# Second MLP of an attention-and-two-MLPs kernel: its matmuls in long runs, its inputs prepared without GpSimd

## The chip, the cores and the metric

The kernel runs on one core of one Trainium2 chip. The time is that of one launch on the device, in microseconds (us), the median of several executions. Engines are called PE or TensorE (matmuls), PEld (TensorE's weight loads, which overlap the matmuls), DVE or VectorE, ACT or ScalarE, POOL or GpSimd, and SP or SyncE, which here only issues DMAs.

## The reference

Attention through a packed set of 32 queries per head, then two MLPs on the 4608 x 512 result, all in float32:

```python
out = sm_attn(q, p_packed, p_packed)          # p_packed = sm_attn(p, k, v); 8 batches, 8 heads, 576 x 64
x = out as (4608, 512)
h = x @ moe_w_in                              # (512, 2048)
x = where(h >= 1, h, where(h <= -1, 0, (h + 1) ** 2 / 4)) @ moe_w_out
h = x @ moe2_w_in                             # second MLP: (512, 2048)
out = (h * 1 / (1 + exp(-h))) @ moe2_w_out    # (2048, 512)
```

The weights come as 64-bit floats, and the kernel turns them into 32-bit ones itself. A float32 product is made of three TensorE passes, each factor being split into a high and a low part (high x high, high x low, low x high).

## The kernel before

**Stages.** Attention and the first MLP run in 256 steps (NA = 256), a step being one (batch, half, column block m) triple: `a_h` makes the hidden block (6 matmuls of 288 columns, L544), four steps ahead of its use; `a_relu`, `a_max`, `a_hi`, `a_lo` make its activation g on ScalarE and VectorE (L552 to L568); `a_y` multiplies it into the output (12 matmuls, L578). The result goes to DRAM as y_dram. Then comes the second MLP.

**The second MLP** works on six blocks of 2 x 384 tokens and, in each, on eight pairs of hidden column blocks; a pair of a block is numbered q, 0 to 47. The hidden values of a pair are a 2 x 2 block product, done with seven products in place of eight. Product j (0 to 6) of pair q is `b_product`: 6 matmuls of 384 columns (L702), a2r (a prepared piece of the first weights, loaded from a_dram by `load_a` on SyncE's queue) times y2 (a prepared side of the block's tokens, made by `b_side` and `split_b`). Products 0, 2, 4 and 6 are written to one PSUM bank, 1, 3 and 5 to another; products 2, 5 and 6 add to what the bank holds, the others start it anew. So between two products on one bank the chain must have read it: `c_sum` (L715 on ScalarE for p1, L722 on VectorE for u2, u3, c22, c21 and c12), or for c11 the sigmoid and the multiply, which read the bank directly. Each of the four hidden blocks c11, c22, c21, c12 then takes a sigmoid (`c_sig`, L728, ScalarE), a multiply (`c_mult`, L733, VectorE), and a split into high (`c_hi`, L737, ScalarE) and low part (`c_lo`, L742, VectorE).

The output product of a pair, `b_out`, has 36 matmuls of 512 columns (L756), into six banks that gather over the eight pairs of a block; at the last pair they are copied to osb tiles and written out. Before the change it is cut into seven parts of 5 or 6 matmuls, and part j of pair q stands behind product j of pair q + 1.

**The second output weights** (key "o2") are read as raw 64-bit words (`load_raw`, SyncE), scaled on ScalarE (`conv_a`, L162), put together on VectorE (`conv_b`, L168 and L169) and split by `conv_c`: ScalarE makes the high part (L206), GpSimd the low part (L207). Before the change nine of the 16 go through from step NA - 10 on, the others every fourth place. The first weights of the second MLP (key "i2") are prepared much earlier, a pair at a time, from step ai = 24 on, every ad = 27 steps, by `conv_a`, `conv_b` and `a_first` to `a_fourth`.

**What sets the order.** Every operation is put down as an event with a number (`ev`, or `at`, which adds 0.6), and the events are written out in the order of these numbers; each engine's queue then runs in that order. kb(q, j) is the place of product j of pair q, one unit a product. The seven low parts of block 0's y2 tiles are made by GpSimd (L664), those of later blocks by VectorE.

## Time and profile before

| | us |
|---|---|
| median of three executions | 1579.46 |
| lowest, highest | 1578.46, 1586.15 |
| profiled execution, whole | 1583.54 |
| its span, first to last instruction | 1581.8 |
| TensorE busy in the span | 1536.6 (97%) |
| VectorE, ScalarE busy | 1041.8 (66%), 683.5 (43%) |
| GpSimd busy | 124.3 (8%) |
| share of TensorE in the chain that ended last | 85% |

TensorE is the engine that is nearly always busy. Matmuls are pipelined: the recorded duration of one reaches beyond the start of the next, so a busy TensorE can still start its matmuls at a faster or a slower rate. How far apart they start has to be read from the order of time: the starts of two rows, or a row's length less one matmul, divided by its count less one.

### The profile page before, as it was taken

What the parts mean: (1) busy time and instruction counts of PE and PEld (TensorE: products, weight loads), DVE (VectorE), ACT (ScalarE), POOL (GpSimd) and SP (SyncE); (2) the same over time, 40 slices, a digit from 0 to 9 for tenths busy, and PEclk for the clock granted to TensorE, in tenths of its full rate; (3) what the DMA queues carried; (4) which work ended last, traced back from release to release, by engine and by line L of the source; (5) the groups of instructions that cost most, each with busy time, mean ns of one, the idle gap of its engine ahead of it and who ended that gap; (6) DMA issues with size and microseconds to landing.
All of it is one profiled execution on the core that took longest, in us unless ns stands there. A gap on an engine that the chain in (4) does not pass through costs nothing.

```text
span 1581.8 us, 26920 instructions
## 1 busy us (share of the span) xinstructions
PE 1536.6 (97%) x10110; PEld 1404.6 (89%) x10110; DVE 1041.8 (66%) x2105; ACT 683.5 (43%) x1479; POOL 124.3 (8%) x138
## 2 busy tenths in 40 slices
PE   6899999999999999999979999999999999999998
PEld 4687899989999999999969988988998998988897
DVE  5998779776868588767685465465456456447444
ACT  4565456454544455534454343243233234224222
POOL 1431310000000000000251000000000000000000
PEclk7999999999999999999999999999999999999999
DMA  9545675183424544213435445355355455455432
GB/s 335 180 171 167 226 254 156 45 248 98 131 97 128 168 143 138 89 43 102 149 124 177 127 146 157 118 157 156 118 155 156 117 160 154 119 155 150 124 118 87
DMA packets 140433, 231.15 MB, mean 146 GB/s; under 512 B 25104, under 2 KB 71184, under 8 KB 140304
## 3 DMA queue, kind: packets, MB, share of 16 engines
q1 hardware_dynamic: 133392, 204.26, 41.0%
q0 software_dynamic: 6912, 25.17, 5.1%
q8 instruction: 81, 1.33, 0.4%
q14 instruction: 48, 0.39, 0.1%
...
## 4 chain that ended last, share of the span: by engine, by line
PE 85%; DVE 9%; ACT 2%; DMA 2%; issue 1%; SPq 0%; POOL 0%; DVEq 0%; ACTq 0%; POOLq 0%
PE ps_o L756 23%; PE ps_y L578 23%; PE ps_h L702 21%; PE ps_h L544 11%; PE ps_wp L514 2%; PE ps_s L375 2%; DVE raw L168 1%; DVE u L557 1%; DVE w L169 1%; PE ps_s L264 1%; DVE u L558 1%; PE ps_pp L338 1%; DVE g L568 1%; DVE w_in L169 1%; DVE y L664 1%
## 5 line engine op out<-in xcount | busy, mean ns | idle before, releaser
L578 PE MATMUL ps_y<-g,w_o 128*128 128x288 f32 x3072 | 462.8, 300 | 9.2 <-DVE g L568 7.3
L756 PE MATMUL ps_o<-w_o,g 128*128 128x512 f32 x1728 | 452.1, 393 | 0.0
L578 PEld LDWEIGHTS ps_y<-g,w_o 128*128 128x128 f32 x3072 | 429.4, 191 | 25.4 <-DVE g L568 8.6
L702 PE MATMUL ps_h<-y,a2r 128*128 128x384 f32 x2016 | 411.2, 339 | 2.9 <-ACT p L715 1.5
L702 PEld LDWEIGHTS ps_h<-y,a2r 128*128 128x128 f32 x2016 | 365.1, 188 | 32.9 <-ACT p L715 5.0
L756 PEld LDWEIGHTS ps_o<-w_o,g 128*128 128x128 f32 x1728 | 319.3, 188 | 47.9
L544 PE MATMUL ps_h<-a,wp 128*128 128x288 f32 x1536 | 248.0, 298 | 4.9 <-DVE u L558 3.9
L552 ACT ACTIVATE u<-ps_h,half 128x288 f32<-128x288 f32 x256 | 128.0, 502 | 257.0 <-PE ps_h L544 192.0
L544 PEld LDWEIGHTS ps_h<-a,wp 128*128 128x128 f32 x1536 | 219.7, 190 | 8.6 <-DVE u L558 5.5
L557 DVE SCALAR_TENSOR_TENSOR u<-u 128x288 f32<-128x288 f32 x256 | 124.3, 486 | 105.7 <-ACT u L552 105.0
L728 ACT ACTIVATE s<-c 128x384 f32<-128x384 f32 x144 | 75.7, 526 | 192.5 <-DVE c L722 192.4
L737 ACT CAST g<-s 128x384 fp32r<-128x384 f32 x192 | 98.5, 513 | 107.4 <-DVE s L733 106.5
L722 DVE TENSOR_TENSOR c<-ps_h,u 128x384 f32<-128x384 f32 x144 | 80.0, 555 | 76.0 <-PE ps_h L702 76.0
L558 DVE TENSOR_TENSOR u<-ps_h,u 128x288 f32<-128x288 f32 x256 | 117.1, 457 | 8.8
L742 DVE TENSOR_TENSOR g<-s,g 128x384 fp32r<-128x384 f32 x192 | 107.5, 560 | 23.3 <-ACT g L737 22.5
L562 ACT CAST g<-u 128x288 fp32r<-128x288 f32 x256 | 109.0, 427 | 19.2 <-DVE u L558 18.3
L568 DVE TENSOR_TENSOR g<-u,g 128x288 fp32r<-128x288 f32 x240 | 116.4, 485 | 0.5
L733 DVE TENSOR_TENSOR s<-c,s 128x384 f32<-128x384 f32 x144 | 80.4, 558 | 47.9 <-ACT s L728 47.9
L728 ACT ACTIVATE s<-ps_h 128x384 f32<-128x384 f32 x48 | 23.6, 492 | 136.9 <-PE ps_h L702 136.8
L733 DVE TENSOR_TENSOR s<-ps_h,s 128x384 f32<-128x384 f32 x48 | 26.7, 557 | 75.9 <-ACT s L728 75.7
L529 DVE TENSOR_TENSOR wp<-ps_wp,wp 64x512 fp32r<-64x512 f32 x96 | 65.7, 687 | 12.5 <-ACT wp L527 10.8
L722 DVE TENSOR_TENSOR u<-ps_h,p 128x384 f32<-128x384 f32 x48 | 26.6, 555 | 54.1 <-PE ps_h L702 54.1
...
## 6 DMA issues: line engine op xcount, KB each, us to landing
a2r<-a_dram SPq DMA_DIRECT2D x336, 256.0 KB, 2.6
...
a_dram<-a2w SPq DMA_DIRECT2D x56, 256.0 KB, 3.5
...
```

What stands on the lines that cost most here:

```text
L544: nc.tensor.matmul(ps[:, :HB], w[:, i, o:o + P], a2[:, k, g, :], start=(n == 0), stop=(n == 3 * NG - 1))
L552: nc.scalar.activation(u, h_ps[s][:, :HB], AF.Relu, bias=half, scale=0.5)
L557: nc.vector.scalar_tensor_tensor(u, u, 1.0, u, op0=ALU.min, op1=ALU.mult)
L558: nc.vector.tensor_tensor(u, h_ps.pop(s)[:, :HB], u, op=ALU.max)
L562: nc.scalar.copy(g[:, 0], u_t[s])
L568: eng.tensor_tensor(g[:, 1], u_t.pop(s), g[:, 0].bitcast(F32), op=ALU.subtract)
L578: nc.tensor.matmul(acc["y"][d][:, :HB], w[:, i, d * P:(d + 1) * P], g[:, k], start=(first and n == 0), stop=(last and n == 2),)
L702: nc.tensor.matmul(ps, w[:, x, a * P:(a + 1) * P], y[:, k, :], start=(n == 0 and j in (0, 1, 3, 4)), stop=(n == 3 * KH - 1), skip_group_ch ...
L722: nc.vector.tensor_tensor(t, ps, sb[q, other], op=ALU.add)
L733: nc.vector.tensor_tensor(u, src, u, op=ALU.mult)
L742: nc.vector.tensor_tensor(g[:, 1], c_t.pop((q, name))[0], g[:, 0].bitcast(F32), op=ALU.subtract)
L756: nc.tensor.matmul(ps, g[:, x, c * P:(c + 1) * P], w[:, k, :], start=(first and (x, k) == PASSES[0]), stop=(last and (x, k) == PASSES[-1]),)
```

## The change

The output product of a pair is no longer cut up: all 36 matmuls stand behind product 3 of the next pair, so TensorE has products 4, 5, 6 of one pair and 0, 1, 2, 3 of the next as one run of 42, and then a run of 36. Its cells come in another order, both halves of one t after each other. The chain's operations are placed anew among the products. Products 0 to 3 of the first pair now stand between the last four output steps of the first MLP. Low parts of y2 and of the second output weights are made by VectorE throughout. Only four output weights are converted ahead of the second MLP, the others in pairs, each in the output run of an earlier pair; so are the sides of later blocks. The first weights are prepared from step 34 on, every 25 steps. Loads are placed accordingly.

```diff
-        nc.gpsimd.tensor_tensor(t[:, 1], w, t[:, 0].bitcast(F32), op=ALU.subtract)
+        eng = nc.gpsimd if key[0] == "o" else nc.vector
+        eng.tensor_tensor(t[:, 1], w, t[:, 0].bitcast(F32), op=ALU.subtract)
...
-        if n < 7:
+        if n < 5:
             t = big.tile([P, 2, KH * P], F32R, tag="big", name="a2r")
...
-            (eng or nc.vector).tensor_tensor(t[:, 1], src[:, a], t[:, 0].bitcast(F32), op=ALU.subtract)
+            nc.vector.tensor_tensor(t[:, 1], src[:, a], t[:, 0].bitcast(F32), op=ALU.subtract)
...
-        u = tmp("s", 2)
+        u = tmp("s", 3)
...
-    def b_out(q, part):
+    def b_out(q):
         i, p = divmod(q, NPR)
-        cells = [(f, t, c, x) for f, t in ((0, 0), (1, 1), (1, 0), (0, 1)) for c in range(TC) for x in PASSES]
-        n = len(cells)
-        for f, t, c, (x, k) in cells[n * part // 7:n * (part + 1) // 7]:
+        order = ((0, 0), (1, 0), (1, 1), (0, 1)) if q + 1 < NPR * NBK else ((0, 0), (1, 1), (1, 0), (0, 1))
+        cells = [(f, t, c, x) for f, t in order for c in range(TC) for x in PASSES]
+        for f, t, c, (x, k) in cells:
...
-                osb = pools["b"].tile([P, DM], F32, tag="osb", name="osb", bufs=3)
-                if c % 2:
+                if t and c < 2 and q + 1 < NPR * NBK:
+                    osb = big.tile([P, DM], F32, tag="big", name="osb")
+                else:
+                    osb = pools["b"].tile([P, DM], F32, tag="osb", name="osb", bufs=3)
+                if c == 1 or c == 2 and t:
...
-            n = NA - 10 + m if m < 9 else NA - 2 + (m - 8) * 4
+            n = NA - 8 + m if m < 4 else kb(m // 2 - 1) + 3.5
...
-            return NA - 1 + 7 * q + j
+            return NA - 3.95 + 7 * q + j
...
-                at(NA - 15 + 2 * j if i == 0 else n - 7 + 1.4 * j, b_side, i, j)
+                if i == 0:
+                    at(NA - 26 + 3 * j, b_side, i, j)
+                else:
+                    ev(n + 7 * (-2, -1, -1, -1, 0, 0, 0)[j] + 3.6 + 0.01 * j, b_side, i, j)
...
-            ev(kb(0, n) - 4 + 0.39, load_a, n)
+            ev(kb(0, n) - (3 if n < 5 else 4.6) + 0.39, load_a, n)
...
                 ev(kb(q, j) + 0.37, b_product, q, j)
-                ev(kb(q + 1, j) + 0.9, b_out, q, j)
+            ev(kb(q + 1, 3) + 0.9, b_out, q)
```

The chain's table (`chain`) is rewritten too; what it does to VectorE's order is shown below.

TensorE, the last pair but one, before: the last three products of pair 47 (L702; ps_h is the bank, y the token side) with parts of pair 46's output product (L756; g is the hidden block) between them.

```order
L756 MATMUL ps_o<-w_o_13_10531,g_16646 128x512 x3
L756 MATMUL ps_o<-w_o_13_10531,g_16669 128x512 x2
L702 MATMUL ps_h_16658<-y_15681,a2r 128x384 x3
L702 MATMUL ps_h_16658<-y_15684,a2r 128x384 x3
L756 MATMUL ps_o<-w_o_13_10531,g_16669 128x512 x5
L702 MATMUL ps_h_16680<-y_15727,a2r 128x384 x3
L702 MATMUL ps_h_16680<-y_15730,a2r 128x384 x3
L756 MATMUL ps_o<-w_o_13_10531,g_16669 128x512 x2
L756 MATMUL ps_o<-w_o_12_10442,g_16689 128x512 x3
L702 MATMUL ps_h_16658<-y_15757,a2r 128x384 x3
L702 MATMUL ps_h_16658<-y_15760,a2r 128x384 x3
L756 MATMUL ps_o<-w_o_12_10442,g_16689 128x512 x6
```

The same place after the change, from pair 47's product 2 on.

```order
L702 MATMUL ps_h_16658<-y_15617,a2r 128x384 x3
L702 MATMUL ps_h_16658<-y_15620,a2r 128x384 x3
L702 MATMUL ps_h_16673<-y_15624,a2r 128x384 x3
L702 MATMUL ps_h_16673<-y_15627,a2r 128x384 x3
L756 MATMUL ps_o<-w_o_12_10834,g_16582 128x512 x9
L756 MATMUL ps_o<-w_o_13_10837,g_16683 128x512 x9
L756 MATMUL ps_o<-w_o_13_10837,g_16654 128x512 x9
L756 MATMUL ps_o<-w_o_12_10834,g_16696 128x512 x9
L702 MATMUL ps_h_16658<-y_15760,a2r 128x384 x3
L702 MATMUL ps_h_16658<-y_15763,a2r 128x384 x3
L702 MATMUL ps_h_16673<-y_15767,a2r 128x384 x3
L702 MATMUL ps_h_16673<-y_15770,a2r 128x384 x3
```

Between a product and the next one on the same bank there is now a single product, except at the output run.

VectorE, one pair of the second MLP before, from u2 on (L722 sums, L733 multiplies, L742 low parts, by the pair's tiles).

```order
L722 TENSOR_TENSOR u2_12095<-ps_h2_12066,p1_12077 128x384
L733 TENSOR_TENSOR s_12112<-ps_h2_12044,s_12112 128x384
L722 TENSOR_TENSOR u3_12130<-ps_h2_12066,u2_12095 128x384
L742 TENSOR_TENSOR g2_12132<-s_12112,g2_12132 128x384
L722 TENSOR_TENSOR c_12150<-ps_h2_12044,u3_12130 128x384
L733 TENSOR_TENSOR s_12152<-c_12150,s_12152 128x384
L722 TENSOR_TENSOR c_12168<-ps_h2_12066,u2_12095 128x384
L742 TENSOR_TENSOR g2_12170<-s_12152,g2_12170 128x384
L733 TENSOR_TENSOR s_12172<-c_12168,s_12172 128x384
L722 TENSOR_TENSOR c_12191<-ps_h2_12044,u2_12095 128x384
L742 TENSOR_TENSOR g2_12193<-s_12172,g2_12193 128x384
L733 TENSOR_TENSOR s_12195<-c_12191,s_12195 128x384
```

The same engine after the change, from sum c22 on: c_12754 is c22, c_12766 c21, c_12782 c12, and u2_12810 belongs to the next pair.

```order
L722 TENSOR_TENSOR c_12754<-ps_h2_12645,u3_12697 128x384
L722 TENSOR_TENSOR c_12766<-ps_h2_12660,u2_12680 128x384
L733 TENSOR_TENSOR s_12756<-c_12754,s_12756 128x384
L722 TENSOR_TENSOR c_12782<-ps_h2_12645,u2_12680 128x384
L733 TENSOR_TENSOR s_12768<-c_12766,s_12768 128x384
L742 TENSOR_TENSOR g2_12771<-s_12756,g2_12771 128x384
L733 TENSOR_TENSOR s_12784<-c_12782,s_12784 128x384
L722 TENSOR_TENSOR u2_12810<-ps_h2_12790,p1_12797 128x384
L742 TENSOR_TENSOR g2_12800<-s_12768,g2_12800 128x384
L742 TENSOR_TENSOR g2_12813<-s_12784,g2_12813 128x384
```

Multiplies and low parts have moved behind the sums that free a bank.

TensorE in the passage before: the last output steps of the first MLP (L578) and the first products.

```order
L578 MATMUL ps_y<-g,w_o_1227 128x288 x12
L578 MATMUL ps_y<-g,w_o_1230 128x288 x12
L578 MATMUL ps_y<-g,w_o_1360 128x288 x12
L578 MATMUL ps_y<-g,w_o_1373 128x288 x12
L702 MATMUL ps_h_10088<-y_9638,a2r 128x384 x3
L702 MATMUL ps_h_10088<-y_9641,a2r 128x384 x3
L578 MATMUL ps_y<-g,w_o_1309 128x288 x12
```

The same place after the change (there the line is L579).

```order
L579 MATMUL ps_y<-g,w_o_1227 128x288 x12
L702 MATMUL ps_h_10003<-y_9336,a2r 128x384 x3
L702 MATMUL ps_h_10003<-y_9339,a2r 128x384 x3
L579 MATMUL ps_y<-g,w_o_1230 128x288 x12
L702 MATMUL ps_h_10032<-y_9423,a2r 128x384 x3
L702 MATMUL ps_h_10032<-y_9426,a2r 128x384 x3
L579 MATMUL ps_y<-g,w_o_1360 128x288 x12
L702 MATMUL ps_h_10003<-y_9507,a2r 128x384 x3
L702 MATMUL ps_h_10003<-y_9510,a2r 128x384 x3
L579 MATMUL ps_y<-g,w_o_1373 128x288 x12
```

A product now stands between each two of the last output steps.

## Rows read from the trace of the kernel before

**Rows 1.** Busy us by stretch: PE, PEld, DVE, ACT, POOL; then granted clock, DMA.

```profile
750.00:780.00 30.00, 30.00 (x228) 30.00 (x227) 17.65 (x40) 11.68 (x30) 2.30 (x3) 1.00 0.32 114
...
796.90:826.60 29.70, 20.23 (x110) 18.24 (x109) 25.31 (x37) 16.65 (x32) 17.02 (x13) 0.89 0.34 111
...
800.00:820.00 20.00, 12.89 (x70) 11.75 (x70) 17.47 (x25) 10.96 (x22) 12.62 (x10) 0.83 0.12 37
...
827.70:1565.20 737.50, 736.81 (x3645) 661.62 (x3645) 395.09 (x732) 255.53 (x515) 7.84 (x6) 1.00 0.47 141
```

**Rows 2.** TensorE in order of time, one period: start, us, line, tiles, count.

```profile
1205.08 1.21 PE L702 MATMUL ps_h<-y,a2r 128*128 128x384 f32 x6
...
1215.00 1.32 PE L756 MATMUL ps_o<-w_o,g 128*128 128x512 f32 x5
...
1220.83 1.21 PE L702 MATMUL ps_h<-y,a2r 128*128 128x384 f32 x6
```

**Rows 3.** TensorE in order of time, longer runs of products and of outputs.

```profile
824.53 2.07 PE L702 MATMUL ps_h<-y,a2r 128*128 128x384 f32 x11
...
1566.25 9.72 PE L756 MATMUL ps_o<-w_o,g 128*128 128x512 f32 x42
...
1568.56 7.42 PE L756 MATMUL ps_o<-w_o,g 128*128 128x512 f32 x32
```

**Rows 4.** TensorE, passage: one y step, then groups (busy, mean ns, idle before, releaser).

```profile
792.14 1.77 PE L578 MATMUL ps_y<-g,w_o 128*128 128x288 f32 x12
...
L578 PE MATMUL ps_y<-g,w_o 128*128 128x288 f32 x60 | 11.3, 344 | 7.3 <-DVE g L568 7.3
L702 PE MATMUL ps_h<-y,a2r 128*128 128x384 f32 x48 | 9.6, 346 | 2.2 <-ACT p L715 1.1 <-DMA a2r<-a_dram 0.6 <-DVE s L733 0.5
```

**Rows 5.** VectorE and ScalarE in order of time, in the period of rows 2.

```profile
1215.20 0.56 DVE L722 TENSOR_TENSOR c<-ps_h,u 128x384 f32<-128x384 f32 x1 [1.19 <-PE ps_h L702]
1216.41 0.56 DVE L733 TENSOR_TENSOR s<-c,s 128x384 f32<-128x384 f32 x1 [0.65 <-ACT s L728]
1217.42 0.56 DVE L722 TENSOR_TENSOR c<-ps_h,u 128x384 f32<-128x384 f32 x1 [0.45 <-PE ps_h L702]
1217.89 0.55 DVE L742 TENSOR_TENSOR g<-s,g 128x384 fp32r<-128x384 f32 x1
...
1215.85 0.52 ACT L728 ACTIVATE s<-c 128x384 f32<-128x384 f32 x1 [3.40 <-DVE c L722]
```

**Rows 6.** All engines in order of time, first products.

```profile
816.84 0.42 DVE L168 TENSOR_SCALAR raw<-raw 128x512 uint32<-128x512 uint32 x1
...
817.39 0.69 DVE L169 SCALAR_TENSOR_TENSOR w<-raw 128x512 uint32<-128x512 uint32 x1
...
820.90 0.56 DVE L733 TENSOR_TENSOR s<-ps_h,s 128x384 f32<-128x384 f32 x1 [1.63 <-ACT s L728]
...
821.51 1.01 PEld L702 LDWEIGHTS ps_h<-y,a2r 128*128 128x128 f32 x6 [0.86 <-DVE s L733]
```

**Rows 7.** Order of time, a weight load that waited and its matmul.

```profile
956.59 0.49 PEld L702 LDWEIGHTS ps_h<-y,a2r 128*128 128x128 f32 x3 [0.15 <-ACT p L715]
...
956.71 0.52 PE L702 MATMUL ps_h<-y,a2r 128*128 128x384 f32 x2
```

**Rows 8.** DMA issues: KB each, median us from issue to landing.

```profile
a2r<-a_dram SPq DMA_DIRECT2D x336, 256.0 KB, 2.6
```

**Rows 9.** Groups on VectorE from 780 to 826: busy, mean ns, idle before.

```profile
L169 DVE SCALAR_TENSOR_TENSOR w<-raw 128x512 uint32<-128x512 uint32 x10 | 11.4, 1138 | 0.9
```

**Rows 10.** Order of time, an early conversion and TensorE's wait behind it.

```profile
158.44 1.02 DVE L168 TENSOR_SCALAR raw<-raw 128x512 uint32<-128x512 uint32 x1
159.49 0.69 DVE L169 SCALAR_TENSOR_TENSOR w<-raw 128x512 uint32<-128x512 uint32 x1
...
162.53 1.12 PE L306 MATMUL ps_et<-ident,s 128*128 128x128 f32 x4 [2.88 <-DVE u L558]
```

More of the change, by code (lines that the diff above doesn't have):

```diff
@@ L658, in load_y, with split_b @@
         yr_t[i, k, t] = yr
-    def split_b(i, j, src, eng=None):
+    def split_b(i, j, src):
         for a in range(KH):
@@ L663, in split_b @@
             nc.scalar.copy(t[:, 0], src[:, a])
-            (eng or nc.vector).tensor_tensor(t[:, 1], src[:, a], t[:, 0].bitcast(F32), op=ALU.subtract)
+            nc.vector.tensor_tensor(t[:, 1], src[:, a], t[:, 0].bitcast(F32), op=ALU.subtract)
             b_t[i, j, a] = t
     def b_side(i, j):
-        eng = nc.gpsimd if i == 0 else nc.vector
         b11, b12, b21, b22 = (yr_t[i, k, t] for k in range(2) for t in range(2))
         if j == 0:
-            split_b(i, 0, b11, eng)
+            split_b(i, 0, b11)
             nc.vector.tensor_tensor(b11, b12, b11, op=ALU.subtract)
@@ L675, in b_side @@
             nc.vector.tensor_tensor(t2, b22, b11, op=ALU.subtract)
-            split_b(i, 1, t2, eng)
+            split_b(i, 1, t2)
             yr_t[i, "t2"] = t2
         elif j == 2:
-            split_b(i, 2, b21, eng)
+            split_b(i, 2, b21)
         elif j == 3:
             nc.vector.tensor_tensor(b12, b22, b12, op=ALU.subtract)
-            split_b(i, 3, b12, eng)
+            split_b(i, 3, b12)
         elif j == 4:
-            split_b(i, 4, b11, eng)
+            split_b(i, 4, b11)
         elif j == 5:
             nc.vector.tensor_tensor(b21, b21, yr_t[i, "t2"], op=ALU.subtract)
-            split_b(i, 5, b21, eng)
+            split_b(i, 5, b21)
         else:
-            split_b(i, 6, b22, eng)
+            split_b(i, 6, b22)
     bk, sb, c_t = {}, {}, {}
@@ L708, in tmp @@
     def tmp(name, bufs):
-        return pools["b"].tile([P, TH], F32, tag=name, name=name, bufs=bufs)
+        return pools["y" if name == "p1" else "b"].tile([P, TH], F32, tag=name, name=name, bufs=bufs)
     def c_sum(q, name):
@@ L772, in b_out @@
                     s0 += m
[L775 removed]
+    G = dict(pf1=4, pb1=18, w1=2, sp0=25, spd=125, pf2=25, pf3=41, pb2=44, pp2=52, t20=52, t21=58, t22=57, t23=65, pbo=7, pfa=18, pfb=25, pbe=40, pp=36, t0=37, t1=53, t2=49, t3=66, lw=3, lk=4, lv=-1, lq=21, ppd=0, ai=34, ad=25, wpd=1, bev=4, oraw=1)
     starts = {b: (0,) if b else (0, KF // 2) for b in range(B)}
@@ L978, in attention_then_two_mlps @@
         at(NA - SPB, start_b)
-        at(NA - 2, end_a)
+        ev(NA - 1.6, end_a)
         for p in range(NPR):
@@ L988, in attention_then_two_mlps, with kb @@
                 at(n + 8 + x, fn, p)
+        def kb(q, j=0):
+            return NA - 3.95 + 7 * q + j
         for m in range(KF):
             key = ("o2", m)
-            n = NA - 10 + m if m < 9 else NA - 2 + (m - 8) * 4
-            at(n - 3, load_raw, key)
-            at(n, conv_a, key)
-            at(n + 1, conv_b, key)
-            at(n + 2, conv_c, key)
-        def kb(q, j=0):
-            return NA - 1 + 7 * q + j
+            n = NA - 8 + m if m < 4 else kb(m // 2 - 1) + 3.5
+            ev(n - 4, load_raw, key)
+            ev(n, conv_a, key)
+            ev(n + (1 if m < 4 else 0.02), conv_b, key)
+            ev(n + (2 if m < 4 else 0.04), conv_c, key)
         for i in range(NBK):
@@ L1003, in attention_then_two_mlps @@
                 for t in range(2):
-                    at((NA - 22 if i == 0 else n - 13) + 2 * k + t, load_y, i, k, t)
+                    ev((NA - 31.4 if i == 0 else n - 22) + 2 * k + t, load_y, i, k, t)
             for j in range(7):
-                at(NA - 15 + 2 * j if i == 0 else n - 7 + 1.4 * j, b_side, i, j)
+                if i == 0:
+                    at(NA - 26 + 3 * j, b_side, i, j)
+                else:
+                    ev(n + 7 * (-2, -1, -1, -1, 0, 0, 0)[j] + 3.6 + 0.01 * j, b_side, i, j)
         for n in range(7 * NPR * NBK):
-            ev(kb(0, n) - 4 + 0.39, load_a, n)
+            ev(kb(0, n) - (3 if n < 5 else 4.6) + 0.39, load_a, n)
         chain = {
-            1: [(c_sum, "p1")],
-            2: [(c_sum, "u2")],
-            3: [(c_sig, "c11"), (c_mult, "c11")],
-            4: [(c_sum, "u3"), (c_hi, "c11"), (c_lo, "c11")],
-            5: [(c_sum, "c22"), (c_sig, "c22"), (c_mult, "c22")],
-            6: [(c_sum, "c21"), (c_hi, "c22"), (c_sig, "c21"), (c_lo, "c22"), (c_mult, "c21")],
-            7: [(c_sum, "c12"), (c_hi, "c21"), (c_sig, "c12"), (c_lo, "c21"), (c_mult, "c12")],
-            8: [(c_hi, "c12"), (c_lo, "c12")],
+            1: [(c_sum, "p1", 0)],
+            2: [(c_sum, "u2", 0)],
+            3: [(c_sig, "c11", 0), (c_mult, "c11", 1), (c_sum, "u3", 2), (c_hi, "c11", 3), (c_lo, "c11", 4)],
+            5: [(c_sum, "c22", 0), (c_sig, "c22", 1)],
+            6: [(c_sum, "c21", 0), (c_sig, "c21", 1), (c_mult, "c22", 2), (c_hi, "c22", 3)],
+            7: [(c_sum, "c12", 0), (c_sig, "c12", 1), (c_mult, "c21", 2), (c_lo, "c22", 3)],
+            8: [(c_mult, "c12", 1), (c_hi, "c21", 2)],
+            9: [(c_lo, "c21", 1), (c_hi, "c12", 2), (c_lo, "c12", 3)],
         }
@@ L1021, in attention_then_two_mlps @@
                 ev(kb(q, j) + 0.37, b_product, q, j)
-                ev(kb(q + 1, j) + 0.9, b_out, q, j)
+            ev(kb(q + 1, 3) + 0.9, b_out, q)
             for j, fns in chain.items():
-                for x, (fn, name) in enumerate(fns):
+                for fn, name, x in fns:
                     ev(kb(q, j) + 0.4 + 0.01 * x, fn, q, name)
```

1 line of the change is left out of this document (removed).

## The prediction

> **What bounds the kernel now.** I read the stretches first, then the order of time, then the waits. In the stage of the second MLP, 827.7 to 1565.2 us, TensorE is busy 736.81 of 737.50 us at a granted clock of 1.00, with VectorE at 395 and ScalarE at 256 [rows 1]. So the stage is bound by the rate at which matmuls start, and a change there pays only through that rate. A period of 42 product and 36 output matmuls takes 15.75 us, from 1205.08 to 1220.83 [rows 2]; the stage holds 3645 / 78 = 46.7 periods [rows 1], of 737.5 / 46.7 = 15.79 us on average, block borders included.
>
> That rate isn't what long runs reach. Eleven products in a row start (2.07 - 0.33) / 10 = 173.6 ns apart, and 32 output matmuls in a row (7.42 - 0.39) / 31 = 226.8 ns apart [rows 3]. At these spacings 42 + 36 matmuls are 7.29 + 8.16 = 15.45 us, 0.30 less than the period of runs of 6 and 5. The run of 42 at the end, taken from its first matmul, has (9.72 - 0.39) / 41 = 227.6 ns [rows 3]: some 41 x 0.8 ns = 0.03 us are lost once at its head. Runs of 5 or 6 pay such a head 14 times a period.
>
> The other place is the passage from the first MLP to the second. From 796.9 to 826.6 TensorE is busy 20.2 of 29.7 us, at a clock of 0.89, 0.83 in its middle [rows 1]. It does 60 matmuls of 288 and 48 of 384 columns; its idle time is mostly VectorE's g, 7.3 us [rows 4]. At the usual (1.77 - 0.30) / 11 = 0.134 us [rows 4] and 0.174 these are 8.0 + 8.4 = 16.4 us, so the passage loses 13.3.
>
> **The change part by part.** *Runs.* A period becomes 15.45 plus a head for each of two runs, 0.03 (measured) and about as much for the products (taken from the same row), so 15.51 if nothing waits. Before, a product's result had an output part of 1.2 us and a product before its bank was written again; now it has one product of 1.04 us, five times a period. Call the products P4 P5 P6 of one pair and P0 to P3 of the next, and count from the start of P4. Handing over costs: product's end to VectorE 0.20 (1215.00 to 1215.20), sum to sigmoid 0.65, sigmoid to multiply 0.56, VectorE 0.56 an operation and 0.47 from one start to the next where they are independent [rows 2, 5]; a VectorE end to the weight load that waits for it 0.05 (821.46 to 821.51), which I take for ScalarE too, and VectorE to its own dependent successor 0.13 (817.26 to 817.39) [rows 6]. A weight load 0.12 us ahead of its matmul costs it nothing (956.59, 956.71) [rows 7].
> P4 ends at 1.07, P5 at 2.11, P6 at 3.15, then P0 4.19, P1 5.23, P2 6.27, P3 7.31. Sum c22 starts 1.27, frees P6's bank at 1.88; wanted at 1.99. Sum c21: 2.31, 2.92; wanted 3.03. Multiply c22 comes behind c21 at 2.78 and ends 3.34; sum c12 takes over its tile, so it starts between 3.47 and 3.52 and frees P1's bank at 4.08 to 4.13; wanted 4.07. The sigmoid of c12 (4.13) holds ScalarE up to 0.52, so copy p1, priced like it, ends by 5.17 and frees P2's at 5.22, or 0.1 sooner where the two overlap; wanted 5.15. Sum u2 starts 5.47, frees P3's at 6.08; wanted 6.19. So c12, and perhaps p1, is late by 0 to 0.10 in a period. I take 0.04, the middle of c12's, which the durations pin best. P4 and P5 (multiply c11, sum u3) have the output run of 8.2 us as cover.
> *Vector work in the output run.* For the first pairs it holds multiply, sum and low half of c11 (3 x 0.56) and two weights, each 0.42 + 0.69 and a subtraction, which I price at 0.69 as the like-sized operation: 5.3 of 8.2 us. Nothing of it is paid for; were it 3 us longer, sum c22 would be late and each us of it would cost a us. Before a block's border three y sides stand there, 6 x 0.56 + 2 x 0.95 for the wider ones (twice 0.47, by columns) + 1.7 = 7.0: still under. At the borders themselves the periods of before are longer, which is in the 15.79; I leave 1 us of that for the five new borders.
> Sum: 47 x (15.79 - 15.51 - 0.04) = 11.3, less 1: **10.3 us**. Bounds: 0.10 late each period and the borders as before (2 us for 1), 6.5; none late and no border cost, 13.2.
> *Loads on SyncE's queue.* a2r lands 2.6 us after its issue [rows 8]. Five buffers hold P4 to P1; P2's load goes out when P4 ends, at about 1.3, and is there by 3.9 to 4.4 with 0.5 allowed for the issue; wanted 5.15. P3's: 5.4, wanted 6.19. The weights' raw loads stand behind P3's load, ahead of P4's, whose product has the output run to come. The output writes stand at the borders ahead of P2's load only. Cost zero; without that slack of 0.8 us P2 would pay what is missing.
> *Passage.* GpSimd's 14 y subtractions and 16 weight subtractions go to VectorE; 12 of 16 weights leave the passage, and 4 y steps are interleaved with P0 to P3. Ten L169 from 780 to 826 took 1138 ns each [rows 9]; the one at 817.39 took 690 [rows 6], and GpSimd, which ran 17 of the passage's 30 us [rows 1], is what it shares the passage with. A step of 18 matmuls takes TensorE 18 x 0.134 = 2.4 us; VectorE's work in one is 17.65 / 30 x 2.4 = 1.4 (750 to 780 us) [rows 1]. In the four steps that hold weights 0.42 + 0.69 + 0.69 come on top: 3.2 against 2.4, and against 1.6 + 1.04 = 2.65 once a product stands in the step. With three steps of the first kind and one of the second that is a lag of 3 us at full durations, 2 where they overlap by 0.1, and g is wanted a step and a half (3.6 us) after its place. From 0 (all covered) to 5 us (lag uncovered, with the sigmoid table's load) remains; I take 2.5, nearer the middle as the y sides before it fill VectorE already. 13.3 - 2.5 = **10.8 us** (8.3 to 13.3).
> *Pairs of the first weights* (ai, ad). Pair 0 moves some ten steps later. Two of its conversions stand ahead of the u for which TensorE waits 2.88 us until 162.53, the second with 1.02 + 0.69 [rows 10]. Without them that wait shrinks by up to its whole length, but the same work lands elsewhere: between 1.7 lost, where that second conversion meets as tight a place, and 2.9 won; I take **1.7** won, that conversion alone.
> The tail keeps its order: 36 output matmuls after the last product, then copies and writes.
> Total 10.3 + 10.8 + 1.7 = 22.8 us. The profiled execution took 1583.54 (span 1581.8): 1560.7. It lies 4.1 above the median, 1579.46, to which the forecast refers: **1557 us**.
>
> **The rivals.** *The handovers are late.* Five a period x 47 = 235. If each is 0.10 us later than worked out above, after its slack, 23.5 us go back: 1580, no change. For: all five have 0.1 us of slack or less. Against: the durations are steady, and a late one shifts all that follows with it. *Much later*: with 0.25 each 59 us: 1614, slower. It decides from 0.13 each, (1587 - 1557) / 235. It would need VectorE to reach the product run with work left over from the output run.
> *The runs don't settle*: small waits renew the head every product, the spacing stays as now, and only passage and start pay: 1567. For: there are five chances for it in a run. Against: the eleven products in a row cross from P6 to P0 [rows 3].
> *The passage stays VectorE-bound*: it takes over 30 subtractions. With 8 us more left: 1565.
> *The clock falls.* It was 0.83 in 800 to 820, where TensorE waited four times for VectorE's g, 7.3 us in all [rows 1, 4]. If the handover waits did the same to the product runs, 7.3 x (1 / 0.83 - 1) = 1.5 us a period, 70 in all: 1627. Against: it stayed at 1.00 through the stage [rows 1]. The Trainium skill (TensorE: Matmul & The Clock Gate, A second HAM failure mode: psum-queue depth-cycling) reports a kernel whose short idle times between groups of matmuls, while it cycled through banks, made the clock swing; that speaks against this change, and no row of before shows it.
> *Long runs go below the samples*, down to their columns at 2.4 GHz, 160 and 213 ns: 14.4 us a period, 1.05 less, 49 in all: 1508. Rows 3 speak against it, 32 in a row without a further fall. The Trainium skill (the same page, Wait — 56ns, not 53.3ns?) gives columns / 2.4 GHz plus about 2.5 ns as the distance of warm matmuls, which is close to that end; by it the period would be 14.6. The trace disagrees by 11 ns a matmul.
>
> **How the numbers follow.** Forecast 0.75; late by 0.10 (1580) 0.07; much later (1614) 0.04; not settling (1567) 0.08; passage (1565) 0.03; clock (1627) 0.02; below the samples (1508) 0.01. About 0.5%, 7.9 us, is what a measurement of this kernel can tell from no change. Faster by more: 0.75 + 0.08 + 0.03 + 0.01 = 0.87; within: 0.07; slower: 0.06. The range holds the forecast with its bounds and the rivals at 1565 and 1567, and leaves out the rest: low, 1557 less 2.9 (runs), 2.5 (passage) and 1.2 (pairs) = 1550.4, taken as 1551; high 1568, just past the rival at 1567 and the other ends of the three terms, 1557 + 3.8 + 2.5 + 3.4 = 1566.7.
>
> **What would show it.** Right: a period near 15.55 us; rows of 42 products with spacings near 174 ns and 36 outputs near 227; TensorE's idle time in the passage under 3 us with the clock at 1.00 and L169 at 0.69; no GpSimd after the first MLP. Wrong: weight loads that wait for c or p in every period; a period at 15.7 or more; VectorE busy up to the end of the output run; TensorE waiting for g in the last steps of the first MLP; or a new wait between 150 and 250 us.

## The result, and the profile after

The changed kernel takes 1560.63 us, the median of four executions (1559.21 to 1562.29); the kernel before, run beside it, 1581.07. The ratio is 0.987, with a 95% interval of 0.984 to 0.990: 1.0 to 1.6% faster. The prediction was 1557, with a range of 1551 to 1568. The profiled execution took 1560.93, where the prediction had worked out 1560.7 for one beside the profiled 1583.54.

So the total fits almost exactly. Its terms don't. The spans of the two profiled executions can be cut at three matmuls that both have: the first of the last five output steps of the first MLP (step 251), the first of product P4 of pair 0 (behind 60 output matmuls and the 24 of P0 to P3 in either kernel), and the last product matmul.

| us, from the starts in order of time | before | after | gained | predicted |
|---|---|---|---|---|
| start to step 251 (first MLP) | 796.93 | 784.30 | 12.6 | 1.7 |
| step 251 to P4 of pair 0 (passage) | 24.58 | 12.33 | 12.2 | 10.8 |
| P4 of pair 0 to the last product | 744.57 | 747.75 | -3.2 | 10.3 |
| last product to the end | 15.70 | 14.78 | 0.9 | 0 |
| span | 1581.8 | 1559.2 | 22.6 | 22.8 |

Before, 42 output matmuls follow the last product, after the change 36 (the prediction took 36 for both). So six of them, 1.4 us, have moved from the fourth row into the third; for equal work the second MLP is 1.8 us slower and the tail 0.5.

The second MLP, for which the runs were made, came out slower by itself. The first MLP gained what is missing there.

TensorE in the passage after, in order of time (start, us, line, tiles, count). The same place as in [rows 4]:

```profile
784.30 1.77 PE L579 MATMUL ps_y<-g,w_o 128*128 128x288 f32 x12
785.90 1.24 PE L702 MATMUL ps_h<-y,a2r 128*128 128x384 f32 x6
786.98 1.78 PE L579 MATMUL ps_y<-g,w_o 128*128 128x288 f32 x12
...
795.03 1.77 PE L579 MATMUL ps_y<-g,w_o 128*128 128x288 f32 x12
796.63 5.40 PE L702 MATMUL ps_h<-y,a2r 128*128 128x384 f32 x30
```

Every one of these rows begins where the one before it runs out, and none has a wait. A step and a product together take 786.98 - 784.30 = 2.68 us. Busy time by stretch (PE, PEld, DVE, ACT, POOL; then granted clock, DMA share, GB/s), which answers [rows 1]:

```profile
780.00:800.00 20.00, 20.00 (x138) 20.00 (x137) 13.96 (x30) 9.47 (x19) 0.00 (x0) 1.00 0.27 84
800.00:820.00 20.00, 19.52 (x101) 17.79 (x100) 13.44 (x26) 9.52 (x20) 0.00 (x0) 1.00 0.67 226
840.00:1500.00 660.00, 651.18 (x3249) 587.67 (x3248) 347.66 (x665) 224.99 (x473) 0.00 (x0) 1.00 0.45 145
```

VectorE has six of 20 us to spare in the passage and the clock stays at 1.00. But in the second MLP TensorE now idles, 8.8 of 660 us, which it did not in [rows 1].

Two periods after, TensorE in order of time (answers [rows 2]):

```profile
1002.10 7.50 PE L702 MATMUL ps_h<-y,a2r 128*128 128x384 f32 x42
1009.43 8.36 PE L756 MATMUL ps_o<-w_o,g 128*128 128x512 f32 x36
1017.64 7.55 PE L702 MATMUL ps_h<-y,a2r 128*128 128x384 f32 x42
1025.02 8.36 PE L756 MATMUL ps_o<-w_o,g 128*128 128x512 f32 x36
```

VectorE's sums in the first of them (answers [rows 5]):

```profile
1003.36 0.56 DVE L722 TENSOR_TENSOR c<-ps_h,u 128x384 f32<-128x384 f32 x1 [8.04 <-PE ps_h L702]
1004.40 0.56 DVE L722 TENSOR_TENSOR c<-ps_h,u 128x384 f32<-128x384 f32 x1 [0.48 <-PE ps_h L702]
...
1005.53 0.56 DVE L722 TENSOR_TENSOR c<-ps_h,u 128x384 f32<-128x384 f32 x1
...
1007.59 0.56 DVE L722 TENSOR_TENSOR u<-ps_h,p 128x384 f32<-128x384 f32 x1
```

The period is 1017.64 - 1002.10 = 15.54 us, against 15.75 before and 15.55 predicted. Counted from the run's start, sum c22 begins at 1.26 (worked out: 1.27), c21 at 2.30 (2.31), c12 at 3.43 (3.47 to 3.52), u2 at 5.49 (5.47). Within a block, then, the runs do what was worked out.

At the five block borders they don't. From P4 to P4 the period there is 17.77, 17.77, 19.45, 16.71 and 17.59 us. The first border after, SyncE's queue (SPq, time of issue):

```profile
920.12 4.00 SPq L774 DMA_DIRECT2D out<-osb  x8
924.21 7.78 SPq L653 DMA_DIRECT2D a2r<-a_dram  x7
```

TensorE over the same time:

```profile
921.91 5.41 PE L702 MATMUL ps_h<-y,a2r 128*128 128x384 f32 x30
929.29 2.35 PE L702 MATMUL ps_h<-y,a2r 128*128 128x384 f32 x12 [1.97 <-DMA a2r<-a_dram]
```

What the DMA engines do meanwhile (share and GB/s are the last two columns of the stretches):

```profile
922.00:924.00 2.00, 2.00 (x13) 2.00 (x12) 0.56 (x1) 0.78 (x3) 0.00 (x0) 1.00 0.99 326
924.00:926.00 2.00, 2.00 (x14) 2.00 (x13) 1.68 (x4) 1.29 (x4) 0.00 (x0) 1.00 0.94 256
926.00:928.00 2.00, 1.32 (x8) 1.00 (x6) 1.87 (x5) 1.81 (x4) 0.00 (x0) 1.00 0.96 304
```

And the group of products from 840 to 1500 us (busy, mean ns, idle before):

```profile
L702 PE MATMUL ps_h<-y,a2r 128*128 128x384 f32 x1753 | 317.2, 338 | 8.8 <-DMA a2r<-a_dram 8.6 <-DVE g L742 0.2
```

The run of 42 breaks after 30 matmuls, P2's load missing. P4 had ended at 921.91 + 1.07 = 922.98 and freed the buffer; the load is issued at 924.21, behind eight output writes of 1.5 MB together, and by the trace lands at 929.15, 4.9 us later, where the median of all these loads is 2.6 before [rows 8] and 3.0 in this kernel. It was wanted 5.15 us into the run, at 927.06.

At the third border the same wait, 2.10 us, is followed by a fall of the granted clock to 0.50, the 1.2 GHz level, from 1185 to 1188 us. It makes that period 1.7 us longer than the first two; the mean of 1.00 over the 660 us above hides it.

```profile
1183.55 3.31 PE L702 MATMUL ps_h<-y,a2r 128*128 128x384 f32 x12 [2.10 <-DMA a2r<-a_dram]
...
1184.00:1188.00 4.00, 4.00 (x15) 3.72 (x14) 1.58 (x3) 1.00 (x2) 0.00 (x0) 0.57 0.38 116
```

### The profile page after: what moved, and what is told of

It reads as the page before. It is cut to its first block, busy times and chain, and to the rows that moved or that the text cites. A ratio compares the mean times of both kernels' runs of the same rounds, so it can differ in the third digit from the quotient of the medians.

```text
span 1559.2 us, 26894 instructions
## 1 busy us (share of the span) xinstructions
PE 1521.1 (98%) x10110; PEld 1396.0 (90%) x10110; DVE 1029.2 (66%) x2129; ACT 677.3 (43%) x1485; POOL 85.9 (6%) x108
## 4 chain that ended last, share of the span: by engine, by line
PE 89%; DVE 6%; DMA 2%; issue 1%; ACT 1%; SPq 0%; POOL 0%; DVEq 0%; ACTq 0%; POOLq 0%
PE ps_o L756 25%; PE ps_y L579 24%; PE ps_h L702 21%; PE ps_h L545 12%; PE ps_wp L515 2%; DMA a2r<-a_dram 2%; PE ps_s L376 2%; DVE raw L168 1%; PE ps_s L265 1%; DVE u L558 1%; DVE w L169 1%; PE ps_pp L339 1%; PE ps_wp L444 1%; DVE u L559 1%; DVE w_in L169 1%
## 5 line engine op out<-in xcount | busy, mean ns | idle before, releaser
L579 PE MATMUL ps_y<-g,w_o 128*128 128x288 f32 x3072 | 457.6, 298 | 1.7 <-ACT g L563 1.0
L579 PEld LDWEIGHTS ps_y<-g,w_o 128*128 128x128 f32 x3072 | 425.1, 189 | 16.7 <-issue 5.7
L756 PE MATMUL ps_o<-w_o,g 128*128 128x512 f32 x1728 | 402.0, 390 | 0.0
L756 PEld LDWEIGHTS ps_o<-w_o,g 128*128 128x128 f32 x1728 | 324.5, 188 | 65.6
L702 PE MATMUL ps_h<-y,a2r 128*128 128x384 f32 x2016 | 365.4, 338 | 9.3 <-DMA a2r<-a_dram 9.1
L702 PEld LDWEIGHTS ps_h<-y,a2r 128*128 128x128 f32 x2016 | 353.6, 188 | 17.0 <-issue 9.0
L722 DVE TENSOR_TENSOR c<-ps_h,u 128x384 f32<-128x384 f32 x144 | 80.3, 558 | 315.8 <-PE ps_h L702 310.8
L742 DVE TENSOR_TENSOR g<-s,g 128x384 fp32r<-128x384 f32 x192 | 102.3, 553 | 4.7
L733 DVE TENSOR_TENSOR s<-c,s 128x384 f32<-128x384 f32 x144 | 79.3, 550 | 0.0
L528 ACT CAST wp<-ps_wp 64x512 fp32r<-64x512 f32 x96 | 55.6, 582 | 5.4 <-PE ps_wp L515 3.4
L495 POOL DMA_DIRECT2D win<-win_dram x48 | 25.6, 534 | 412.7 <-PE ps_wp L515 127.4
L162 ACT ACTIVATE raw<-raw 128x512 f32<-128x512 f32 x64 | 42.7, 681 | 5.5 <-DMA raw<-w_out 3.2
```

The source lines that it names most:

```text
L579: nc.tensor.matmul(acc["y"][d][:, :HB], w[:, i, d * P:(d + 1) * P], g[:, k], start=(first and n == 0), stop=(last and n == 2),)
L702: nc.tensor.matmul(ps, w[:, x, a * P:(a + 1) * P], y[:, k, :], start=(n == 0 and j in (0, 1, 3, 4)), stop=(n == 3 * KH - 1), skip_group_ch ...
L722: nc.vector.tensor_tensor(t, ps, sb[q, other], op=ALU.add)
L742: nc.vector.tensor_tensor(g[:, 1], c_t.pop((q, name))[0], g[:, 0].bitcast(F32), op=ALU.subtract)
L756: nc.tensor.matmul(ps, g[:, x, c * P:(c + 1) * P], w[:, k, :], start=(first and (x, k) == PASSES[0]), stop=(last and (x, k) == PASSES[-1]),)
```

## The experiments

Two theories were at stake for the second MLP: the border loss is the writes' place ahead of the load, or it is something that the long runs bring with them at a border. For the passage: GpSimd's removal, or the spreading of the work. For the first MLP: the pairs of first weights, or the other edits. All results (median; the kernel before beside it on the same chip; ratio with its 95% interval), and the profiled spans cut as above:

| run | us | before | ratio | to step 251 | to P4 | to last product |
|---|---|---|---|---|---|---|
| changed kernel | 1560.63 | 1581.07 | 0.987 (0.984-0.990) | 784.3 | 12.33 | 747.75 |
| after_again | 1561.61 | 1581.12 | 0.987 (0.985-0.989) | 785.6 | 12.34 | 747.80 |
| e1_pairs_alone | 1572.38 | 1579.84 | 0.996 (0.994-0.997) | 786.3 | 24.61 | 745.17 |
| e2_pairs_undone | 1567.11 | 1579.84 | 0.993 (0.991-0.995) | 792.0 | 12.34 | 743.71 |
| e4_writes_gpsimd | 1571.59 | 1579.84 | 0.995 (0.994-0.997) | 784.2 | 12.33 | 752.99 |
| e9_loads_ahead | 1550.50 | 1579.84 | 0.982 (0.981-0.983) | 786.9 | 12.34 | 735.72 |
| e5_runs_undone | 1577.85 | 1581.44 | 0.998 (0.997-0.999) | 785.3 | 12.34 | 761.96 |
| e6_gpsimd_back | 1559.83 | 1581.44 | 0.986 (0.985-0.988) | 782.8 | 12.34 | 744.57 |
| e7_before_no_gpsimd | 1578.01 | 1581.44 | 0.998 (0.997-0.999) | 796.3 | 22.16 | 745.77 |
| e8_one_more_sum | 1577.56 | 1581.44 | 0.998 (0.996-0.999) | 786.4 | 12.34 | 763.11 |
| e10_writes_later | 1548.99 | 1581.12 | 0.980 (0.978-0.981) | 784.6 | 12.34 | 735.78 |
| e11_loads_ahead_start | 1547.84 | 1581.12 | 0.979 (0.977-0.980) | 784.3 | 12.34 | 734.38 |
| e12_products_after_y | 1557.56 | 1581.12 | 0.986 (0.983-0.988) | 783.7 | 13.65 | 742.81 |

The last three columns are of one execution each, and the last one varies by itself: the second MLP of e2 is the changed kernel's, and took 743.71 us in place of 747.75. Part of that is the clock at the third border.

### The borders: e4, e9, e10

```diff
-                    nc.sync.dma_start(out[...], osb[z:z + m])
+                    nc.gpsimd.dma_start(out[...], osb[z:z + m])
```

> The changed kernel with the output writes issued on GpSimd's queue, which is idle in the second MLP, in place of SyncE's. At the five block borders the changed kernel loses 10 to 11 us (periods of 16.7 to 18.8 in place of 15.55). If the loss is that P2's load stands behind eight output writes on SyncE's queue (4 us of issue and their semaphores), it goes: 7 to 10 us below the changed kernel (1551 to 1554). If the loss is that the writes' 1.5 MB occupy the DMA engines while the load is under way, it stays: within 2 us of 1560.6.

It got 11 us slower than the changed kernel; neither number was met. TensorE at the first border in e4:

```profile
927.78 1.28 PE L702 MATMUL ps_h<-y,a2r 128*128 128x384 f32 x6 [0.44 <-DMA a2r<-a_dram]
931.75 2.26 PE L702 MATMUL ps_h<-y,a2r 128*128 128x384 f32 x6 [2.69 <-DMA a2r<-a_dram]
933.80 10.08 PE L756 MATMUL ps_o<-w_o,g 128*128 128x512 f32 x36
```

Busy time and clock of the stretches there:

```profile
922.00:928.00 6.00, 5.56 (x32) 5.26 (x31) 4.10 (x9) 3.88 (x9) 2.92 (x6) 1.00 0.95 265
928.00:932.00 4.00, 1.31 (x7) 1.02 (x7) 1.49 (x4) 1.00 (x2) 0.00 (x0) 0.83 0.97 338
932.00:934.00 2.00, 2.00 (x7) 2.00 (x8) 0.00 (x0) 0.00 (x0) 0.00 (x0) 0.50 0.21 73
```

P2's load now goes out at 923.18, at once when P4 ends, and still needs until 927.64, 4.5 us; P3's takes from 924.22 to 931.61, 7.4 us. The DMA engines are at 0.95 to 0.97. So the queue was only part of the delay: writes from another queue fill the same engines, and the last of them lands at 931.4 here, at 927.2 in the changed kernel. The Trainium skill (DMA: Bandwidth & Descriptors, Issuing engines are not separate DMA queues) says that transfers of all issuing engines run on the same 16 DMA engines and interleave; this trace agrees. The rest of the 11 us: the clock falls to 0.50 (1.2 GHz) during the second wait, the output run takes 9.9 us there and at another border, and the last writes end 21.0 us after the last product in place of 14.8.

```diff
-        if n < 5:
+        if n < 5 or n > 63 and n % 56 in (9, 10):
             t = big.tile([P, 2, KH * P], F32R, tag="big", name="a2r")
...
-            ev(kb(0, n) - (3 if n < 5 else 4.6) + 0.39, load_a, n)
+            ev(kb(0, n) - (3 if n < 5 else 6.6 if n > 63 and n % 56 in (9, 10) else 4.6) + 0.39, load_a, n)
```

> The changed kernel with the loads of products 2 and 3 of the pair behind a block border issued two places earlier, ahead of the output writes, into two more buffers. If the border loss is the load's late issue: TensorE has no wait for a2r there, the five long periods come down to about 15.6 to 15.7, and the time is 8 to 10 us below the changed kernel (1551 to 1553). If something else holds TensorE at the borders (the copies of the six banks, the y sides on VectorE), the wait for the load goes and another one of like length takes its place: within 2 us of 1560.6.

Met: 1550.50, a second MLP of 735.72, and at the borders nothing took the wait's place. But e9 changes two things, the order and the number of buffers. e10 changes the order, and beside it only the pool of one osb tile; it puts the writes back instead of the loads forward:

```diff
+            ev(kb(q + 1, 5) + 0.8, write_out)
...
-                    nc.sync.dma_start(out[...], osb[z:z + m])
+                    o_late.append((out[...], osb[z:z + m]))
```

> The changed kernel with the border's output writes put behind the loads of products 2 and 3 on SyncE's queue (one and a half places later; one more osb tile comes from the large pool so that no copy waits for a write). The loads' own places and buffers stay. If the writes ahead are the whole border loss, by queue and DMA engines together: P2's load goes out when P4 ends and lands in some 2.6 us, the wait for a2r goes, and the time is 8 to 10 us below the changed kernel run beside it. If the buffer comes free too late in any case (five buffers): the wait only shrinks, and the gain is under 4 us.

12.6 us below the changed kernel beside it, more than expected. SyncE's queue at the same border in e10:

```profile
914.87 10.62 SPq L653 DMA_DIRECT2D a2r<-a_dram  x3
925.54 5.40 SPq L748 DMA_DIRECT2D out<-osb  x8
```

TensorE there:

```profile
922.88 7.49 PE L702 MATMUL ps_h<-y,a2r 128*128 128x384 f32 x42
930.21 8.36 PE L761 MATMUL ps_o<-w_o,g 128*128 128x512 f32 x36
```

And its group of products from 840 to 1500 us:

```profile
L702 PE MATMUL ps_h<-y,a2r 128*128 128x384 f32 x1772 | 317.6, 337 | 0.0
```

P2's load goes out at 924.13 and lands at 926.82, 2.7 us later; the run of 42 is whole, and no product waits in 660 us. Five buffers are enough; what cost the time is that the writes stood ahead.

### The start of the second MLP: e11

```diff
-        if n < 5 or n > 63 and n % 56 in (9, 10):
+        if n < 7 or n > 63 and n % 56 in (9, 10):
...
-(3 if n < 5 else 6.6 if ...
+(3 if n < 5 else 4.9 if n < 7 else 6.6 if ...
```

> The kernel of the earlier run with the border loads ahead, and the same for the first pair: products 5 and 6 load into two more of the large buffers, a little sooner. The earlier run still waits 1.3 us for a2r in the first product run (804 us). If that wait goes and nothing takes its place: about 1 us below that run, 10 to 11 us below the changed kernel run beside it. If VectorE or ScalarE are as late there: the same as that run.

1547.84, 13.8 us below the changed kernel beside it, more than expected; by its trace the second MLP is 1.3 us shorter than in e9. Its stretches, for those of the changed kernel above, leave TensorE next to no idle time:

```profile
800.00:820.00 20.00, 20.00 (x104) 18.48 (x104) 14.14 (x29) 9.79 (x21) 0.00 (x0) 1.00 0.66 230
...
840.00:1500.00 660.00, 659.96 (x3310) 597.66 (x3309) 350.99 (x673) 226.78 (x477) 0.00 (x0) 1.00 0.47 147
```

It is 2.1% below the kernel before (2.0 to 2.3%) and the fastest version here. It and e10, 1.15 us apart, can't be told apart by their times.

### What the runs are worth, and how thin their cover is: e5, e8

```diff
-            ev(kb(q + 1, 3) + 0.9, b_out, q)
+                ev(kb(q + 1, j) + 0.9, b_out, q, j)
```

> The changed kernel with the output product cut into seven parts again, one behind each product, in the order of cells of before; all else stays. If the runs are worth what the prediction says (0.24 us a period) and the borders cost some 10 us only because of the runs: the period returns to 15.75, the waits for a2r at the borders go, and the two cancel, so the time is within 3 us of the changed kernel's 1560.6. If the runs are worth nothing by themselves and the borders' cost stays: 1560 too, but with long borders in the trace. If the prediction's 10.3 us net stood: 1571.

16 to 17 us above the changed kernel: all three numbers missed. TensorE in e5, ahead of a border:

```profile
1037.63 1.23 PE L702 MATMUL ps_h<-y,a2r 128*128 128x384 f32 x6
1038.69 1.32 PE L757 MATMUL ps_o<-w_o,g 128*128 128x512 f32 x5
1041.89 1.31 PE L702 MATMUL ps_h<-y,a2r 128*128 128x384 f32 x6 [1.87 <-DVE c L722]
```

Within a block the period is back at 15.75, 0.20 more than with runs, as expected: 47 x 0.20 = 9.4 us. The waits for a2r are gone too. But the y sides, which the change bunches between products 3 and 4, now have no run of 8.2 us over them: sum c22 comes 1.87 us late, and the two periods at a border are 17.9 and 17.0 us. At the first border the period ahead is long too (17.6), and at the fourth the clock falls to 0.50 behind the same wait. In all the borders lose 20.1 us over periods of 15.75, against 11.5 over 15.55 in the changed kernel. These 8.6 and the 9.4 are more than the 14.2 us by which its second MLP is longer: six output matmuls, 1.4 us, stand behind the last product here and ahead of it there, and the changed kernel lost another 2.4 us in its first period and in periods between the borders. So the run is also the cover for the new places of VectorE's work, and this experiment undoes the one without the other.

```diff
-            6: [(c_sum, "c21", 0), (c_sig, "c21", 1), ...
+            6: [(c_sum, "c21", 0), (c_dummy, "p1", 1), (c_sig, "c21", 1), ...
```

> The changed kernel with one needless VectorE addition (128x384, into the dead p1 tile) between sum c21 and multiply c22 of each pair, 0.47 us from start to start, ahead of sum c12, whose bank the prediction found free 0.01 to 0.06 us late. If the cover is as thin as worked out, each of the 48 periods gets 0.40 to 0.47 us longer: 19 to 23 us above the changed kernel (1580 to 1584), with weight loads that wait for VectorE's sum. If the chain has slack that the working did not see (a later bank, matmuls that wait in the queue), less: within 8 us.

16 to 17 us above the changed kernel, between the two numbers and nearer the first. TensorE's product runs in order of time:

```profile
1007.91 4.35 PE L702 MATMUL ps_h<-y,a2r 128*128 128x384 f32 x24
1012.43 3.41 PE L702 MATMUL ps_h<-y,a2r 128*128 128x384 f32 x18 [0.16 <-DVE c L722]
...
1023.88 7.95 PE L702 MATMUL ps_h<-y,a2r 128*128 128x384 f32 x42
...
1039.87 4.36 PE L702 MATMUL ps_h<-y,a2r 128*128 128x384 f32 x24
```

And the weight loads of the products from 840 to 1500 us, with their waits:

```profile
L702 PEld LDWEIGHTS ps_h<-y,a2r 128*128 128x128 f32 x1708 | 299.1, 189 | 29.9 <-DVE c L722 14.8 <-ACT g L740 7.7 <-issue 2.4
```

A period is 1039.87 - 1023.88 = 15.99 us, 0.44 more than without the added sum: of its 0.47 us nearly all goes to the path, so behind sum c21 the cover is as thin as worked out. Over 47 periods that is 20 us. The borders give 3.8 of it back: they lose 7.7 us over 15.98 here, 11.5 over 15.55 in the changed kernel, with waits for a2r of 7.0 and 8.6 us in the stage. The second MLP is 15.4 us longer.

### The passage: e6, e7, e12

```diff
-        eng = nc.gpsimd if key[0] == "o" else nc.vector
+        eng = nc.vector if key[0] == "i2" else nc.gpsimd
...
-            nc.vector.tensor_tensor(t[:, 1], src[:, a], ...
+            (nc.vector if i else nc.gpsimd).tensor_tensor(t[:, 1], src[:, a], ...
```

> The changed kernel with the low parts of block 0's y2 tiles and of the 16 output weights made by GpSimd again, in their new places. If GpSimd beside VectorE is what made the passage slow (L169 took 1138 ns in it and 690 without), TensorE waits for g or for the products' inputs there again and the time is 4 to 8 us above the changed kernel (1565 to 1569), with L169 over 1000 ns where GpSimd works. If the spreading of the work and the interleaved products are what counts: within 2 us of 1560.6.

Within 1 to 2 us of the changed kernel, and the passage is 12.34 us: with the work spread out, GpSimd costs no time.

```diff
-        nc.gpsimd.tensor_tensor(t[:, 1], w, ...
+        eng = nc.gpsimd if key[0] == "o" else nc.vector
+        eng.tensor_tensor(t[:, 1], w, ...
...
-        eng = nc.gpsimd if i == 0 else nc.vector
+        eng = nc.vector
```

> The kernel before with VectorE in place of GpSimd for these low parts, in the old places (one part of the change alone). VectorE gets 14 + 16 subtractions of 0.5 to 0.7 us and its L169 fall from 1138 to about 690 ns. If the spreading counts, the passage stays bound by VectorE: 2 us below to 6 us above the kernel before (1578 to 1586). If GpSimd was the cause, the passage's 13 us of loss shrink by half without any spreading: 5 to 7 us below (1573 to 1575).

3.4 us below before, by ratio 0.1 to 0.3%, and 2.4 us in the passage: between the two ranges. Groups from 780 to 826 (busy, mean ns, idle before), for [rows 4] and [rows 9]:

```profile
L579 PE MATMUL ps_y<-g,w_o 128*128 128x288 f32 x142 | 22.7, 311 | 5.1 <-DVE g L569 5.1
L169 DVE SCALAR_TENSOR_TENSOR w<-raw 128x512 uint32<-128x512 uint32 x10 | 6.9, 693 | 0.3
L168 DVE TENSOR_SCALAR raw<-raw 128x512 uint32<-128x512 uint32 x10 | 4.2, 421 | 0.0
```

L169 is down from 1138 to 693 ns, as expected, yet TensorE still waits 5.1 us for g: the passage stays bound by VectorE, which now has GpSimd's subtractions.

```diff
-            return NA - 3.95 + 7 * q + j
+            return NA - 1 + 7 * q + j
```

> The changed kernel with the first products behind the last output step of the first MLP, as before, not between the last four; four output weights ahead of them, all on VectorE, stay as changed. By the prediction's working VectorE falls some 3 us behind in the steps that hold weights, 1 us a step of which a product covers: without the products the wait for g in the last steps is 2 to 4 us and the time as much above the changed kernel run beside it. If the twelve weights that left the passage are all that counts: within 1.5 us of it.

No loss: 4 us below the changed kernel beside it, with intervals that overlap; by the traces the difference lies in the second MLP (742.81 us, as low as in e2), not here. The passage is 1.3 us longer, but the row says why:

```profile
783.74 6.79 PE L579 MATMUL ps_y<-g,w_o 128*128 128x288 f32 x48
...
797.39 2.84 PE L702 MATMUL ps_h<-y,a2r 128*128 128x384 f32 x15 [0.96 <-DMA a2r<-a_dram]
```

Four output steps follow each other without any wait for g; what waits is a load. So neither GpSimd's absence (e6) nor the interleaved products (e12) made the gain there by itself. What is left is the twelve weights that went behind the passage and block 0's y sides, which the change starts earlier. No run separates these two, or takes back GpSimd and the interleaving together. By the amount of work it is mostly the weights: between the two cuts VectorE spends 13.3 us on weights and 3.2 on y sides in e7, and 2.5 and nothing in the changed kernel.

### The first MLP: e1, e2

```diff
-ai=24, ad=27
+ai=34, ad=25
```

> The kernel before with one part of the change alone: the first weights' pairs start at step 34 and follow every 25 steps (in place of 24 and 27). The trace after is 12.6 us ahead by the last y step of the first MLP, where the prediction had 1.7. If the pairs' places are the cause, by themselves, this run is 11 to 13 us below the kernel before (1568 to 1570), TensorE's 3.5 us wait near 159 us is gone and the second MLP is as before. By the prediction's term: 1.7 us below (1579). If the gain comes from the other edits of the change (where the last steps and the output weights stand), this run stays within 2 us of before.

> The changed kernel with that part undone (pairs from step 24, every 27). If the pairs' places alone make the gain of the first MLP: 11 to 13 us above the changed kernel (1572 to 1574), with the waits near 159 and 258 us back. By the prediction's term: 1562. If it is tied to the other edits: in between, and e1 and e2 don't add up to one number.

The change of these two numbers by itself is worth 7.5 us by the medians; undone in the changed kernel it costs 5.5 to 6.5, and 7.7 us by step 251. Less than the trace comparison had suggested, three to four times what was predicted. The wait of [rows 10] in e2, where it is back:

```profile
161.58 0.65 PE L307 MATMUL ps_et<-ident,s 128*128 128x128 f32 x4 [2.88 <-DVE u L559]
```

It is the same 2.88 us as before; after the change no row from 150 to 250 us has a wait like it. Further ones near 257 (0.32 and 0.51 us) and 425 us are gone or smaller too, for example this one of before, with later pairs' `a_first` to `a_fourth` on VectorE ahead of it:

```profile
427.12 0.96 PE L514 MATMUL ps_wp<-win,pps 128*128 128x512 f32 x3 [1.43 <-DVE u L558]
```

Of the 12.6 us of the trace comparison 1.3 lie ahead of step 24, before any pair. The other 11.3 are in e1's trace as well: it gains 11.3 us on before from step 24 to 251, with the pairs' places alone. Part of what this exceeds the 5.5 to 7.5 of the medians by is the clock behind these waits. Stretches of before, then of e2:

```profile
155.00:165.00 10.00, 6.40 (x34) 4.38 (x33) 8.87 (x20) 5.69 (x13) 3.56 (x2) 0.84 0.45 158
165.00:175.00 10.00, 10.00 (x131) 9.47 (x130) 5.95 (x11) 3.62 (x8) 2.71 (x2) 0.82 0.31 114
```

```profile
155.00:165.00 10.00, 6.53 (x44) 4.58 (x43) 7.96 (x18) 5.00 (x12) 3.56 (x2) 1.00 0.36 120
165.00:175.00 10.00, 10.00 (x143) 9.47 (x143) 9.58 (x21) 5.46 (x12) 2.71 (x2) 1.00 0.61 223
```

And of e7, the third trace with the pairs in their old places:

```profile
155.00:165.00 10.00, 7.12 (x37) 5.14 (x36) 8.21 (x18) 5.00 (x12) 3.56 (x2) 0.80 0.37 128
165.00:175.00 10.00, 10.00 (x134) 9.47 (x132) 6.64 (x13) 4.02 (x9) 2.72 (x2) 0.86 0.38 137
```

The same wait, and in before the clock is 0.84 and 0.82, in e2 1.00; steps 30 and 31 take 8.8 us there and 6.6 in e2. Near 425 us it costs 1.4 more in the same way. In e7 the clock falls at both places as in before; in none of the eleven traces with the later places does it fall there. So this loss belongs to the waits that the change removes, but not every execution has it. These 3.6 us are most of the 4.1 by which the profiled 1583.54 lay above the median, and e7's profiled execution, with the same falls, lies 3.7 above its own; whether the executions at the median were without them is not shown.

## Why the prediction was right, and where not

**Runs, within a block: right.** 15.55 us a period was forecast, 15.54 is read, and the times of the sums agree to 0.1 us. The handovers behind sum c21 have no cover to spare, as said (e8; those of c22 and c21 themselves were not tried), and none is late by more than the forecast.

**Runs, at the borders: wrong.** The step "the output writes stand at the borders ahead of P2's load only. Cost zero", with its landing of 2.6 us from [rows 8], is the one that failed, and with it "I leave 1 us" for the five borders; they cost 11.5 us, (17.77 + 17.77 + 19.45 + 16.71 + 17.59) - 5 x 15.55, of which 1.7 are the clock's fall at the third border; in the executions of e2 and after_again, with the same borders, they cost 8.4 and 7.8. The landing time is a median over all 336 loads; behind 1.5 MB of writes it is 4.9 us, and from P4's end to the issue behind the eight writes another 1.2 pass. The step even gave the condition, "without that slack of 0.8 us P2 would pay what is missing", and then did not work out the one place where the slack is gone. With the writes behind the loads the second MLP gains 744.57 - 735.78 = 8.8 us (e10) or 10.2 (e11), and 1.4 more for equal work: the 10.3 of the sum was a fair price for runs without this wait.

**Passage: right in size, not in its reasons.** 12.2 us, inside 8.3 to 13.3. By the prediction's own cut, up to the 48th product matmul, it is 29.7 us before and 16.5 after: 13.2 gained, with next to nothing of the loss left. The lag of VectorE that the sum charged with 2.5 us did not come (e12: none even without the interleaved products), and GpSimd's absence, by which L169 was priced, gives 2.4 us alone (e7) and nothing once the work is spread (e6). How the gain divides between the weights and the earlier y sides stays open.

**Pairs: wrong, by a factor of three to four.** 5.5 to 7.5 us where 1.7 stood, with bounds of -1.7 to 2.9. The step priced the part of one wait that one conversion makes, though eight pairs move; all of that wait went, and the later pairs' waits near 257 and 425 us, and the slower clock behind such waits, were not counted.

**The total** is therefore right by luck: between the two profiled executions the missed border loss and the undervalued pairs, with the slower clock in that of before, cancel within 0.2 us. Between the medians the gain is 1581.07 - 1560.63 = 20.4 us, where the forecast had 1579.46 - 1557 = 22.5.

**Rivals.** The handovers were not late, and the runs settled. The clock did fall in the stage, but once, for 3 us behind a wait for a load and not behind the handovers, and it cost 1.7 us and not 70. The spacings stayed at the samples, (1009.43 - 1002.10) / 42 = 174.5 ns a product and 8.21 / 36 = 228 an output, heads included. None of the rivals had a late load at a border; a transfer that loses its cover was the missing one.
